# The second product of a token MLP: weight sums by additions alone, two of four made by an adding transfer

## The chip, the core and the metric

The kernel runs on one core of a Trainium2 chip. The core has a matrix engine (TensorE, PE in the profile, with its weight loads as PEld), a vector engine (VectorE, DVE), an activation engine (ScalarE, ACT), a general one (GpSimd, POOL) and SyncE (SP), which here only issues DMAs. Each engine takes its instructions in order and waits on semaphores for the others. SBUF is the on-chip memory with 128 partitions, PSUM the one into which PE accumulates. The metric is the device time of one execution in microseconds.

## The reference, cut to what matters

```python
def _B_ref(x, w1, b1, w2, b2):
    h = _layernorm(x, axis=-1)                       # (B, S, D)
    u = jnp.einsum("bsd,sf->bdf", h, w1) + b1        # (B, D, F)
    u = _gelu(u)
    y = jnp.einsum("bdf,fs->bds", u, w2) + b2        # (B, D, S)
    return y.transpose(0, 2, 1)

h = x + _A_ref(_layernorm(x), A_wqkv, A_w_phi, A_wo)     # attention
h2 = h + _B_ref(_layernorm(h), B_w1, B_b1, B_w2, B_b2)   # token MLP
```

Here S = 2048 tokens, D = 512 channels, F = 1792 hidden units, all in float32. The change is in the second product of the MLP, `u @ w2`.

## The kernel before, in words

The attention comes first, then the first product of the MLP (w1, lines 62 to 64 through `fill`), then the second (w2, line 789). All large products are made from float32 numbers split into two parts: `split` (lines 55 to 58) lets ACT round a tile to a high part (line 57) and another engine subtract it to get a low part (line 58); three matmuls then take the place of one (high by high, high by low, low by high).

The second product uses a scheme with seven block products in place of eight. The blocks are 2 x 2: the hidden units are taken in NP = 7 pairs of 128 (index `p`), the tokens in 8 pairs of 128 (index `sp`), the channels in two halves HD = 256. For each `sp` and `p` (one of 56 steps, `STEPS`, line 763) the four 128 x 128 blocks of w2 and their sums make seven weight tiles, `raw[:, i, 0]` to `raw[:, i, 6]`. The operands from `u` have their own sums, made once (`operands_u`, lines 729 to 749; for the first two `p` on POOL). `PROD` (line 784) says which weight tile meets which operand and in which of four PSUM banks the product is added. A step is 7 products of 3 matmuls.

`stream_w2` (lines 767 to 781) brings the weights of GRP = 2 steps, a group, so there are 28 groups: two loads from SP's queue (line 773), four additions or subtractions on DVE (lines 777 to 780), and a split of all seven tiles of both steps at once, ACT for `whi`, DVE for `wlo` (lines 57 and 58 through line 781). `raw` has three buffers, `whi` and `wlo` two each. The additions are kept behind one of the last low parts of w1 (`issue_after`, line 776).

After the seventh step of an `sp`, ACT and DVE combine the four banks (lines 820 to 826) into `ot`, and POOL's queue issues two transfers that add the rows to `out` in memory (line 827), which already holds `h`. The last `sp` adds in SBUF instead (`hb`, lines 830 to 847) and stores plainly.

The attention and the first part of w1's product keep an order written out by hand. From there on (line 697 closes the hand-kept stretch) the order on each engine is not written by hand: a planner lays them out when the program is built, by its own estimate of when each becomes ready. Each engine then keeps that order, whatever the real times are. The buffers of a tile are reused only after the last reader of the former content.

Of the kernel before, what the change touches and what calls it, by code (L numbers as in the profile page):

```python
# [9 lines left out]
F32 = mybir.dt.float32  # L10
F32R = mybir.dt.float32r
AF = mybir.ActivationFunctionType
ALU = mybir.AluOpType
# [4 lines left out]
P = 128  # L18
S, D, H, DH, F = 2048, 512, 32, 16, 1792
NT = S // P  # L20
KD = D // P
NF = F // P
NG = 8
NPR = 2 * NG
Q_AT = (4, 6, 8, 9, 11, 13)
# [8 lines left out]
def block_kernel(ctx: ExitStack, tc: tile.TileContext, x, xT, wT, phic, wo, w1, b1, w2, b2,  # L34
                 kvmask, ident_in, out):
    nc = tc.nc
# [7 lines left out]
    mhalf = cst.tile([P, 4], F32, name="mhalf")  # L44
    b1s = cst.tile([P, NF], F32, name="b1s")
    b2s = cst.tile([P, NT], F32, name="b2s")
# [41 lines left out]
    wvl = wp.tile([P, KD, D], F32R, name="wvl")  # L88
    zacc = wp.tile([P, NG, P], F32, name="zacc")
    ps_k = a1.enter_context(tc.tile_pool(name="ps_k", bufs=2, space=PSUM))  # L90
# [75 lines left out]
    def run(*lists):  # L166
        for op in turns(*lists):
            op()
# [7 lines left out]
    def k_ops(t, o):  # L176
        PK[t] = kk.tile([P, NG, P], F32, name="pk", bufs=len(V_NOT) + 3)
        run(logit_ops(o, PK[t], False))
# [187 lines left out]
    def q_logits(lag):  # L366
        n = q["logits"]
        if n < min(NT, q["mm"] - lag + NT * (q["mm"] == NT)):
            EQ[n] = big.tile([P, NG, P], F32, name="eq", tag="big")
            q["logits"] += 1  # L370
# [28 lines left out]
    for t in range(3, NT - 1):  # L399
        if t + 2 < NT:  # L400
            raw = load_x(t + 2)
# [38 lines left out]
    def s_ez(t):  # L440
        EZ[t] = az.tile([P, NG, P], F32, name="ez")
        nc.gpsimd.tensor_mul(EZ[t], EQ[t], zB)  # L442
# [40 lines left out]
    negate()  # L483
    zB = big.tile([P, NG, P], F32, name="zB", tag="big")
    for g in range(2):
# [106 lines left out]
        split(HN[t][:, 0], HN[t][:, 1], hn, nc.gpsimd)  # L592

    w1v = w1.rearrange("(k p) f -> p k f", p=P)
    w2v = w2.rearrange("(k p) s -> p k s", p=P)

    LATER = []

# [15 lines left out]
    PU, WI, LO = {}, {}, []  # L614
    FN, FL = [0] * (NF // 2), [0] * (NF // 2)

# [90 lines left out]

    NP = NF // 2  # L710
    HD = D // 2
    up = ctx.enter_context(tc.tile_pool(name="up", bufs=1, side="right", reuse_waits="tile"))
    uo = ctx.enter_context(tc.tile_pool(name="uo", bufs=2, side="right", reuse_waits="tile"))
    ws = ctx.enter_context(tc.tile_pool(name="ws", bufs=2, side="right", reuse_waits="tile"))
# [3 lines left out]
    NEAR = 2  # L718
    near = [up.tile([P, 7, 2, HD], F32R, name=f"un{p}") for p in range(NEAR)]
    up.tile([P, 120], F32, name="pad")  # L720
    U, UB, far = {}, {}, {}

    def gelu(f, pu):
        if f % 2 == 0:
            U[f // 2] = ur.tile([P, 4, HD], F32, name="u")
        nc.scalar.activation(U[f // 2][:, f % 2 * 2:f % 2 * 2 + 2].rearrange("p k d -> p (k d)"), pu,
                             AF.Gelu_apprx_tanh, bias=b1s[:, f:f + 1])

    def operands_u(p):
        u = U[p]  # L730
        tt = ut.tile([P, 3, HD], F32, name="tt")
        e = nc.gpsimd if p < NEAR else nc.vector
# [11 lines left out]
        for m in range(7):  # L744
            at = (p - NEAR) * 7 + m
            if at % 2 == 0:
                far[at // 2] = big.tile([P, 2, 2, HD], F32R, name="uf", tag="big")
            UB[p, m] = far[at // 2][:, at % 2]
            split(UB[p, m][:, 0], UB[p, m][:, 1], u[:, m] if m < 4 else tt[:, m - 4], nc.vector)

    for p in range(NP):
        while FN[p] < NT:
# [3 lines left out]
        if p < NEAR:  # L756
            operands_u(p)
    for p in range(NEAR, NP):
        operands_u(p)
    wst.close()  # L760
    hp = ctx.enter_context(tc.tile_pool(name="hp", bufs=1, reuse_waits="tile"))

    STEPS = [(sp, p) for sp in range(NT // 2) for p in range(NP)]
    GRP = 2
    AW = {}

    def stream_w2(n):
        steps = STEPS[n:n + GRP]
        raw = ws.tile([P, GRP, 7, P], F32, name="wraw", bufs=3)
        wh_ = ws.tile([P, GRP, 7, P], F32R, name="whi")  # L770
        wl_ = ws.tile([P, GRP, 7, P], F32R, name="wlo")
        for i, (sp, p) in enumerate(steps):
            nc.sync.dma_start(raw[:, i, 0:4].rearrange("p (k i) s -> p k (i s)", k=2),
                              w2v[:, 2 * p:2 * p + 2, sp * 2 * P:(sp + 1) * 2 * P])
            AW[sp, p] = wh_[:, i], wl_[:, i]
        with tc.issue_after(LO[-18]):
            nc.vector.tensor_add(raw[:, :, 4], raw[:, :, 0], raw[:, :, 2])
            nc.vector.tensor_sub(raw[:, :, 0], raw[:, :, 1], raw[:, :, 0])
            nc.vector.tensor_sub(raw[:, :, 5], raw[:, :, 4], raw[:, :, 1])
            nc.vector.tensor_sub(raw[:, :, 6], raw[:, :, 3], raw[:, :, 5])  # L780
        split(wh_, wl_, raw, nc.vector)


# [7 lines left out]
    def products(sp, ps, order):  # L791
        for a, b, bk, half, opens in order:
            for p in ps:
                wh_, wl_ = AW[sp, p]
                product(bank[bk][:, half], (wh_[:, a], wl_[:, a]), UB[p, b], p == 0 and opens, p == NP - 1)

    def flat(a):
        return a.rearrange("p k d -> p (k d)")

    for n, (sp, p) in enumerate(STEPS):  # L800
        t = 2 * sp
        last = t + 2 == NT
        if n % GRP == 0:
            stream_w2(n)
        if p == 0:
            pools = [ps_f, ps_f, ps_q, ps_q] if sp % 2 else [ps_b] * 4
            bank = [pool.tile([P, 2, HD], F32, name="py", tag="pu") for pool in pools]
        if p < NP - 1 - last:
            products(sp, [p], PROD)
            continue  # L810
        if p < NP - 1:
            continue
        by_bank = sorted(PROD, key=lambda m: m[2:4])
        e = uo.tile([P, 2, HD], F32, name="e")
        u2 = uo.tile([P, HD], F32, name="u2", bufs=1)
        u3 = uo.tile([P, HD], F32, name="u3")
        if not last:
            products(sp, [p], by_bank)
            ot = uo.tile([P, 2, 2, HD], F32, name="ot", bufs=1)
            nc.scalar.activation(e[:, 1], bank[0][:, 0], AF.Copy)  # L820
            nc.vector.tensor_add(u2, bank[0][:, 1], e[:, 1])
            nc.vector.tensor_add(u3, bank[1][:, 0], u2)
            nc.vector.tensor_add(e[:, 0], bank[2][:, 0], u2)
            for i, add in enumerate((u3.unsqueeze(1).to_broadcast([P, 2, HD]), e)):
                nc.vector.scalar_tensor_tensor(ot[:, i], bank[2 + i], b2s[:, t + i:t + i + 1], add,  # L825
                                               op0=ALU.add, op1=ALU.add)
                nc.gpsimd.dma_start(out[(t + i) * P:(t + i + 1) * P, :], flat(ot[:, i]), accum_op=ALU.add)  # L827
            continue

        hb = [hp.tile([P, 2, HD], F32, name=f"hb{i}") for i in range(2)]  # L830
        for i in range(2):
            nc.sync.dma_start(flat(hb[i]), out[(t + i) * P:(t + i + 1) * P, :])
            nc.vector.tensor_scalar(hb[i], hb[i], b2s[:, t + i:t + i + 1], None, op0=ALU.add)
        products(sp, [p - 1, p], by_bank)
        nc.scalar.activation(e[:, 1], bank[0][:, 0], AF.Copy)
        nc.vector.tensor_add(hb[1][:, 1], bank[0][:, 0], hb[1][:, 1])
        nc.vector.tensor_add(u2, bank[0][:, 1], e[:, 1])
        nc.vector.tensor_add(hb[1][:, 0], u2, hb[1][:, 0])
        nc.vector.tensor_add(u3, bank[1][:, 0], u2)
        nc.vector.tensor_add(hb[0], hb[0], u3.unsqueeze(1).to_broadcast([P, 2, HD]))  # L840
        nc.vector.tensor_add(hb[0][:, 0], bank[2][:, 0], hb[0][:, 0])
        nc.vector.tensor_add(hb[1][:, 0], bank[2][:, 0], hb[1][:, 0])
        nc.vector.tensor_add(hb[0][:, 1], bank[2][:, 1], hb[0][:, 1])
        nc.sync.dma_start(out[t * P:(t + 1) * P, :], flat(hb[0]))
        for k, q in ((0, nc.scalar), (1, nc.sync)):
            nc.vector.tensor_add(hb[1][:, k], bank[3][:, k], hb[1][:, k])
            q.dma_start(out[(t + 1) * P:NT * P, k * HD:(k + 1) * HD], hb[1][:, k])


def _layout(A_x, A_wqkv, A_w_phi, A_wo, B_w1, B_b1, B_w2, B_b2):  # L850
    x = np.asarray(A_x)[0]
    wqkv = np.asarray(A_wqkv)
    phi = np.asarray(A_w_phi)

    phic = np.concatenate([phi.reshape(4, P, DH).transpose(1, 0, 2).reshape(P, 64),
                           np.kron(np.eye(8), np.ones((DH, 1)))], axis=1).astype(np.float32)
    mask = np.zeros((P, 64), np.float32)
    for a in range(P // DH):
        for c in range(2):
            f = (2 * c + a % 2) * DH  # L860
            mask[a * DH:(a + 1) * DH, f:f + DH] = 1.0

    wo = np.asarray(A_wo).reshape(2, 4, 2, 32, D).transpose(2, 0, 1, 3, 4).reshape(D, D)
    return {
        "x": x,
        "xT": x.reshape(NT, P, KD, P).transpose(0, 3, 2, 1),
        "wT": wqkv.T,
        "phic": phic,
        "wo": wo,
        "w1": np.asarray(B_w1),  # L870
        "b1": np.asarray(B_b1).reshape(NF, P).T,
        "w2": np.asarray(B_w2),
        "b2": np.asarray(B_b2).reshape(NT, P).T,
        "kvmask": mask,
        "ident": np.eye(P, dtype=np.float32),
    }
# [18 lines left out]
```

## Time and profile before

| | |
|---|---|
| median of 3 runs | 534.46 us (534.25 to 535.26) |
| span of the profiled execution, first to last instruction | 532.6 us |
| second product's matmuls begin, busy without a gap | 386.0 us, 138.25 us |
| PE, DVE, ACT, POOL busy, of the span | 98%, 72%, 51%, 44% |
| DMA traffic | 55.81 MB, 105 GB/s on average |
| adding stores of `out` from POOL's queue | 14 of 256 KB, 4.8 us to landing |

The profile is of one execution; the runs are timed without it, and the difference of 1.8 us between the median and the span lies before the first and behind the last instruction. A row of a group reads: line, engine, operation, output<-inputs by the program's names, shapes, count, then busy time and mean duration in ns, then the engine's idle time just before, with what ended it. A row of the timeline begins with start and duration in us; a bracket at its end tells of idle time before it and what ended that. "A <- B: x, n, m" in the waits says that A waited for B for x us in all, n times, m at the longest. Queue q1 is SP's, q0 POOL's; a queue's row has packets, MB and the time its packets took as a share of the time of all 16 DMA engines.

### The profile page before, as it was taken

To read this page: it belongs to the slowest core of one execution; us is meant where nothing else is said; L and a number is where in the kernel's file an instruction comes from. 1 tells how busy PE (TensorE), PEld (TensorE's weight loads), DVE (VectorE), ACT (ScalarE), POOL (GpSimd) and SP (SyncE) were. 2 spreads that over 40 slices of the span, in tenths; PEclk is the share of its full clock that TensorE was granted. 3 is DMA by queue.
4 is the path that set the end of the run, shared out by engine and by line. 5 is a ranking of instruction groups with operands and counts; after the bars stand their busy time and mean duration, and the time that the engine had idled before them with its cause. 6 is when DMAs were issued, how large, how long until landed. Compare 5 with 4: busy or idle time off the path is not lost.

```text
span 532.6 us, 9386 instructions
## 1 busy us (share of the span) xinstructions
PE 520.8 (98%) x3616; PEld 448.7 (84%) x3616; DVE 384.4 (72%) x680; ACT 271.9 (51%) x460; POOL 234.8 (44%) x190
## 2 busy tenths in 40 slices
PE   8999999999999989999999999999999999999995
PEld 7888888886877767777788888888899999999995
DVE  6993999877699989875325524835668877887784
ACT  6998844424336776557746423525444243343340
POOL 2589699877889988887325000000001101100110
PEclk9999999999999999999999999999999999999999
DMA  8633310020502233334255333542014556535631
GB/s 309 206 110 118 99 22 21 1 72 9 160 0 79 82 101 116 104 116 136 85 176 159 98 100 98 159 117 82 20 41 107 143 148 153 123 120 136 143 75 46
DMA packets 45486, 55.81 MB, mean 105 GB/s; under 512 B 3969, under 2 KB 33025, under 8 KB 45441
## 3 DMA queue, kind: packets, MB, share of 16 engines
q1 hardware_dynamic: 43136, 51.38, 30.7%
q0 software_dynamic: 2016, 3.67, 5.5%
q8 instruction: 28, 0.46, 0.4%
q10 hardware_dynamic: 288, 0.17, 0.1%
q14 instruction: 18, 0.14, 0.1%
HBM read 46.81 MB, written 8.39 MB: 104 GB/s over the span
## 4 chain that ended last, share of the span: by engine, by line
PE 83%; POOL 9%; DVE 3%; ACT 2%; issue 1%; DVEq 0%; POOLq 0%; ACTq 0%
PE py L789 26%; PE pu L62 11%; PE pu L63 11%; PE pu L64 11%; POOL ez L442 4%; POOL eq L460 3%; PE pv L63 2%; PE pv L64 2%; PE pv L62 2%; PE pk_ps L62 2%; PE pk_ps L63 2%; PE pk_ps L64 2%; POOL hs L58 2%; PE po L62 1%; PE kvp L207 1%; PE po L63 1%
## 5 line engine op out<-in xcount | busy, mean ns | idle before, releaser
L827 POOL DMA_DIRECT2D out<-ot x14 | 12.5, 1001 | 212.2 <-DVE ot L825 212.2
L789 PE MATMUL py<-uf,whi 128*128 128x256 f32 x560 | 96.2, 283 | 0.0
L63 PE MATMUL pu<-hs,whi 128*128 128x512 f32 x224 | 87.6, 391 | 1.8 <-POOL hs L58 1.8
L602 DVE TENSOR_TENSOR wlo<-wraw,whi 128x512 fp32r<-128x512 f32 x56 | 50.3, 903 | 51.8 <-ACT whi L610 50.7
L57 ACT ACTIVATE whi<-wraw 128x1792 fp32r<-128x1792 f32 x28 | 47.7, 1705 | 77.9 <-PE py L789 73.8
L62 PE MATMUL pu<-hs,whi 128*128 128x512 f32 x224 | 87.4, 395 | 0.0
L64 PE MATMUL pu<-hs,wlo 128*128 128x512 f32 x224 | 87.2, 390 | 0.0
L789 PEld LDWEIGHTS py<-uf,whi 128*128 128x128 f32 x560 | 83.3, 192 | 0.0
L789 PE MATMUL py<-uf,wlo 128*128 128x256 f32 x280 | 69.9, 283 | 0.0
L58 DVE TENSOR_TENSOR wlo<-wraw,whi 128x1792 fp32r<-128x1792 f32 x28 | 56.6, 2022 | 15.4 <-ACT whi L57 15.4
L610 ACT ACTIVATE whi<-wraw 128x512 fp32r<-128x512 f32 x56 | 35.0, 627 | 47.0 <-PE pu L63 44.8
L63 PEld LDWEIGHTS pu<-hs,whi 128*128 128x128 f32 x224 | 42.1, 188 | 11.0 <-POOL hs L58 2.8
L62 PEld LDWEIGHTS pu<-hs,whi 128*128 128x128 f32 x224 | 42.0, 188 | 10.9 <-issue 2.5
L64 PEld LDWEIGHTS pu<-hs,wlo 128*128 128x128 f32 x224 | 42.0, 188 | 9.1 <-DVE wlo L602 0.4
L789 PEld LDWEIGHTS py<-uf,wlo 128*128 128x128 f32 x280 | 49.7, 192 | 0.0
L442 POOL TENSOR_TENSOR ez<-eq,zB 128x1024 f32<-128x1024 f32 x16 | 40.9, 2559 | 2.5 <-ACT zB L488 2.5
L789 PE MATMUL py<-un,whi 128*128 128x256 f32 x224 | 38.4, 283 | 0.0
L195 POOL TENSOR_TENSOR pk<-pk,sk 128x1024 f32<-128x1024 f32 x16 | 31.0, 1941 | 9.8 <-DVE sk L194 9.0
L460 POOL TENSOR_TENSOR eq<-eq,w 128x1024 f32<-128x1024 f32 x16 | 32.0, 1997 | 4.0 <-DVE w L457 4.0
L789 PEld LDWEIGHTS py<-un,whi 128*128 128x128 f32 x224 | 33.2, 192 | 0.1
L199 POOL TENSOR_TENSOR zacc<-zacc,pk 128x1024 f32<-128x1024 f32 x13 | 31.3, 2405 | 0.6
L58 POOL TENSOR_TENSOR hs<-hn,hs 128x512 fp32r<-128x512 f32 x16 | 21.4, 1340 | 17.5 <-ACT hs L57 15.6
(165 smaller groups left out, 1176.5 us busy)
## 6 DMA issues: line engine op xcount, KB each, us to landing
wraw<-in_w SPq DMA_DIRECT2D x112, 256.0 KB, 2.9
xraw<-in_xT SPq DMA_DIRECT2D x16, 256.0 KB, 3.1
xh<-in_x SPq DMA_DIRECT2D x16, 256.0 KB, 2.6
h<-in_x SPq DMA_DIRECT2D x16, 256.0 KB, 2.7
out<-h SPq DMA_DIRECT2D x16, 256.0 KB, 3.0
out<-ot POOLq DMA_DIRECT2D x14, 256.0 KB, 4.8
wraw<-in_wT SPq DMA_DIRECT2D x12, 256.0 KB, 5.0
wo<-in_wo SPq DMA_DIRECT2D x4, 256.0 KB, 3.6
```

The lines of the kernel that those rows point to most:

```text
L57: nc.scalar.activation(hi, src, AF.Copy)
L58: lo_engine.tensor_sub(lo, src, hi)
L62: nc.tensor.matmul(o, ah, bh, start=first, stop=False)
L63: nc.tensor.matmul(o, ah, bl, start=False, stop=False)
L64: nc.tensor.matmul(o, al, bh, start=False, stop=last)
L195: nc.gpsimd.tensor_mul(heads(PK[t]), heads(PK[t]), sk.unsqueeze(2).to_broadcast([P, 2 * H, DH]))
L199: nc.gpsimd.tensor_add(zacc, zacc, PK[t])
L442: nc.gpsimd.tensor_mul(EZ[t], EQ[t], zB)
L460: nc.gpsimd.tensor_mul(heads(EQ[t]), heads(EQ[t]), W[t].rearrange("p g c h -> p (g c h)").unsqueeze(2).to_broadcast([P, 2 * H, DH]))
L602: LO.append(nc.vector.tensor_sub(wl_, raw, wh_).ins)
L610: nc.scalar.activation(wh_, raw, AF.Copy)
L789: nc.tensor.matmul(o, a[x], b[:, y], start=start and i == 0, stop=stop and i == 2, skip_group_check=True)
```

## The change

The sums of weights are formed with other signs, so that all four are additions; the signs are turned back where the banks are combined. Two of the four sums are no longer made by DVE: an adding transfer, issued from POOL's queue, reads blocks 1 and 2 of w2 again from memory and adds them to tiles 0 and 4 in SBUF, after SP's queue has loaded block 0 a second time into tile 4. w2 is laid out in memory beforehand so that a group is one piece of 4 KB in each partition, `raw` has the two steps side by side in its last dimension and a fourth buffer, and the space set aside for the descriptors of POOL's queue is given as 8192.

```diff
 def stream_w2(n):
-    steps = STEPS[n:n + GRP]
-    raw = ws.tile([P, GRP, 7, P], F32, name="wraw", bufs=3)
-    wh_ = ws.tile([P, GRP, 7, P], F32R, name="whi")
-    wl_ = ws.tile([P, GRP, 7, P], F32R, name="wlo")
-    for i, (sp, p) in enumerate(steps):
-        nc.sync.dma_start(raw[:, i, 0:4].rearrange("p (k i) s -> p k (i s)", k=2),
-                          w2v[:, 2 * p:2 * p + 2, sp * 2 * P:(sp + 1) * 2 * P])
-        AW[sp, p] = wh_[:, i], wl_[:, i]
+    g = n // GRP
+    raw = ws.tile([P, 7, GRP * P], F32, name="wraw", bufs=4)
+    wh_ = ws.tile([P, 7, GRP * P], F32R, name="whi")
+    wl_ = ws.tile([P, 7, GRP * P], F32R, name="wlo")
+    nc.sync.dma_start(raw[:, 0:4], w2[g])
+    nc.sync.dma_start(raw[:, 4], w2[g, :, 0])
+    nc.gpsimd.dma_start(raw[:, 0:5:4], w2[g, :, 1:3], accum_op=ALU.add)
+    for i, step in enumerate(STEPS[n:n + GRP]):
+        AW[step] = wh_[:, :, i * P:(i + 1) * P], wl_[:, :, i * P:(i + 1) * P]
     with tc.issue_after(LO[-18]):
-        nc.vector.tensor_add(raw[:, :, 4], raw[:, :, 0], raw[:, :, 2])
-        nc.vector.tensor_sub(raw[:, :, 0], raw[:, :, 1], raw[:, :, 0])
-        nc.vector.tensor_sub(raw[:, :, 5], raw[:, :, 4], raw[:, :, 1])
-        nc.vector.tensor_sub(raw[:, :, 6], raw[:, :, 3], raw[:, :, 5])
+        nc.vector.tensor_add(raw[:, 5], raw[:, 4], raw[:, 1])
+        nc.vector.tensor_add(raw[:, 6], raw[:, 3], raw[:, 5])
     split(wh_, wl_, raw, nc.vector)
...
         nc.scalar.activation(e[:, 1], bank[0][:, 0], AF.Copy)
-        nc.vector.tensor_add(u2, bank[0][:, 1], e[:, 1])
-        nc.vector.tensor_add(u3, bank[1][:, 0], u2)
-        nc.vector.tensor_add(e[:, 0], bank[2][:, 0], u2)
+        nc.vector.tensor_sub(u2, bank[0][:, 1], e[:, 1])
+        nc.vector.tensor_sub(u3, u2, bank[1][:, 0])
+        nc.vector.scalar_tensor_tensor(e[:, 0], bank[2][:, 0], -1.0, u2, op0=ALU.mult, op1=ALU.subtract)
...
     nc.vector.tensor_add(hb[1][:, 1], bank[0][:, 0], hb[1][:, 1])
-    nc.vector.tensor_add(u2, bank[0][:, 1], e[:, 1])
-    nc.vector.tensor_add(hb[1][:, 0], u2, hb[1][:, 0])
-    nc.vector.tensor_add(u3, bank[1][:, 0], u2)
+    nc.vector.tensor_sub(u2, bank[0][:, 1], e[:, 1])
+    nc.vector.tensor_sub(hb[1][:, 0], hb[1][:, 0], u2)
+    nc.vector.tensor_sub(u3, u2, bank[1][:, 0])
...
-    nc.vector.tensor_add(hb[1][:, 0], bank[2][:, 0], hb[1][:, 0])
+    nc.vector.tensor_sub(hb[1][:, 0], hb[1][:, 0], bank[2][:, 0])
...
+    w2 = np.asarray(B_w2).reshape(NP, 2, P, NT // 2, 2, P).transpose(3, 0, 2, 1, 4, 5)
+    w2 = w2.reshape(-1, GRP, P, 4, P).transpose(0, 2, 3, 1, 4).reshape(-1, P, 4, GRP * P)
...
-    nc = bacc.Bacc("TRN2", target_bir_lowering=False, num_devices=1)
+    nc = bacc.Bacc("TRN2", target_bir_lowering=False, num_devices=1, dynamic_dma_scratch_size=8192)
```

More of the change, by code (lines that the diff above doesn't have):

```diff
@@ L22 @@
 NF = F // P
+NP = NF // 2
+HD = D // 2
+GRP = 2
 NG = 8
@@ L594, in block_kernel @@
     w1v = w1.rearrange("(k p) f -> p k f", p=P)
-    w2v = w2.rearrange("(k p) s -> p k s", p=P)
     LATER = []
@@ L699, in block_kernel @@
     aq.close()
-    NP = NF // 2
-    HD = D // 2
     up = ctx.enter_context(tc.tile_pool(name="up", bufs=1, side="right", reuse_waits="tile"))
@@ L763, in block_kernel @@
     STEPS = [(sp, p) for sp in range(NT // 2) for p in range(NP)]
-    GRP = 2
     AW = {}
     def stream_w2(n):
-        steps = STEPS[n:n + GRP]
-        raw = ws.tile([P, GRP, 7, P], F32, name="wraw", bufs=3)
-        wh_ = ws.tile([P, GRP, 7, P], F32R, name="whi")
-        wl_ = ws.tile([P, GRP, 7, P], F32R, name="wlo")
-        for i, (sp, p) in enumerate(steps):
-            nc.sync.dma_start(raw[:, i, 0:4].rearrange("p (k i) s -> p k (i s)", k=2),
-                              w2v[:, 2 * p:2 * p + 2, sp * 2 * P:(sp + 1) * 2 * P])
-            AW[sp, p] = wh_[:, i], wl_[:, i]
+        g = n // GRP
[7 more added lines that the diff above has]
+            AW[step] = wh_[:, :, i * P:(i + 1) * P], wl_[:, :, i * P:(i + 1) * P]
         with tc.issue_after(LO[-18]):
-            nc.vector.tensor_add(raw[:, :, 4], raw[:, :, 0], raw[:, :, 2])
-            nc.vector.tensor_sub(raw[:, :, 0], raw[:, :, 1], raw[:, :, 0])
-            nc.vector.tensor_sub(raw[:, :, 5], raw[:, :, 4], raw[:, :, 1])
-            nc.vector.tensor_sub(raw[:, :, 6], raw[:, :, 3], raw[:, :, 5])
+            nc.vector.tensor_add(raw[:, 5], raw[:, 4], raw[:, 1])
+            nc.vector.tensor_add(raw[:, 6], raw[:, 3], raw[:, 5])
         split(wh_, wl_, raw, nc.vector)
@@ L871, in _layout @@
         "b1": np.asarray(B_b1).reshape(NF, P).T,
-        "w2": np.asarray(B_w2),
+        "w2": w2,
         "b2": np.asarray(B_b2).reshape(NT, P).T,
```

## The prediction

> **What bounds the kernel now.** I read the page's busy shares first, then the chain of work that ended last in order of time, then the busy time by stretches.
>
> ```profile
> span 532.6 us, 9386 instructions
> PE 520.8 (98%) x3616; PEld 448.7 (84%) x3616; DVE 384.4 (72%) x680; ACT 271.9 (51%) x460; POOL 234.8 (44%) x190
> 385.99 138.25 PE py L789 x1152
> 386.00:524.30 138.30, 138.30 (x1154) 138.30 (x1154) 106.83 (x166) 50.06 (x43) 12.48 (x14) 1.00 0.48 115
> 524.30:532.60 8.30, 2.80 (x24) 2.60 (x22) 3.96 (x10) 0.35 (x1) 0.00 (x0) 0.90 0.18 64
> ```
>
> The columns of the last two rows are the stretch, its length, the busy time of PE, weight loads, DVE, ACT and POOL, then granted clock, busy share of the 16 DMA engines and GB/s. The second product is the chain's row at 385.99: 1152 matmuls in 138.25 us, 0.120 us each, PE busy all through at a granted clock of 1.00. DVE has 31 us to spare there, POOL 126. Nothing taken from DVE can shorten this stage; the change can leave it alone or make PE wait. A step has 7 x 3 = 21 matmuls, a group of two steps 42, so 5.04 us; an `sp` has 7 steps, 17.6 us or 3.5 groups. Group g starts at 386 + 5.04 g.
>
> How the weights are fed is seen in the waits of that stretch and in the order of DVE:
>
> ```profile
> ACT whi L57 <- PE py L789: 73.8, 25, 3.3
> DVE wraw L777 <- DMA wraw<-in_w: 11.5, 7, 3.3
> ```
>
> ```profile
> 335.17 2.02 DVE L58 TENSOR_TENSOR wlo<-wraw,whi 128x1792 fp32r<-128x1792 f32 x1 [0.50 <-ACT whi L57]
> ...
> 392.68 2.03 DVE L58 TENSOR_TENSOR wlo<-wraw,whi 128x1792 fp32r<-128x1792 f32 x1 [1.68 <-ACT whi L57]
> ...
> 412.89 2.03 DVE L58 TENSOR_TENSOR wlo<-wraw,whi 128x1792 fp32r<-128x1792 f32 x1 [0.93 <-ACT whi L57]
> 416.40 0.43 DVE L777 TENSOR_TENSOR wraw<-wraw 128x256 f32<-128x256 f32 x1 [1.49 <-DMA wraw<-in_w]
> ...
> 418.00 2.02 DVE L58 TENSOR_TENSOR wlo<-wraw,whi 128x1792 fp32r<-128x1792 f32 x1
> ```
>
> ACT rounds a group's weights to `whi` only when PE has left the buffer of two groups before; DVE makes `wlo` behind it and so frees `raw`. The first `wlo` here is that of group 0; the next three are those of groups 2, 6 and 7. The one that ends at 414.92 is 1.3 us ahead of group 6 (416.24). At 416.40 DVE stood 1.49 us in front of the sums of group 8, waiting for their load, with the `wlo` of group 7 queued behind. That cost nothing, because its `whi` was only just ready; a longer way to the sums makes just this wait longer.
>
> **The change part by part.** *Work on DVE.* A group loses two of its four sums.
>
> ```profile
> L777 DVE TENSOR_TENSOR wraw<-wraw 128x256 f32<-128x256 f32 x23 | 9.7, 421 | 11.6 <-DMA wraw<-in_w 11.5
> L821 DVE TENSOR_TENSOR u<-py,e 128x256 f32<-128x256 f32 x7 | 2.9, 417 | 0.0
> L825 DVE SCALAR_TENSOR_TENSOR ot<-py,b2s,u 128x512 f32<-128x512 f32 x7 | 5.2, 744 | 0.0
> ```
>
> Two at 0.42 us are 0.84 us a group, 23.5 us over 28 groups, all beside a PE that is never idle: worth 0. The turned signs at the end of an `sp` put a subtraction for an addition of the same size (0.417); the one new form with a scalar lies between 0.42 and the 0.744 of twice the columns, at most 0.33 x 7 = 2.3 us of DVE's spare time. That is also its price if the cover were gone. Behind the last matmul there are as many operations as before: 0.
>
> *Transfers.* SP issued two loads of 256 KB a group and now issues one of 512 and one of 128 KB, again two, so nothing more stands ahead of w1's loads in its queue. New is the adding transfer of 256 KB from POOL, which waits for both. DMA time is priced from the page's queues:
>
> ```profile
> q1 hardware_dynamic: 43136, 51.38, 30.7%
> q0 software_dynamic: 2016, 3.67, 5.5%
> 394.73 113.64 SPq L773 DMA_DIRECT2D wraw<-in_w  x46
> L827 POOL DMA_DIRECT2D out<-ot x14: 858/1075/1227, 408.1 to 515.1; - x14
> wraw<-in_w SPq DMA_DIRECT2D x112, 256.0 KB, 2.9
> h<-in_x SPq DMA_DIRECT2D x16, 256.0 KB, 2.7
> ```
>
> SP's queue: 30.7% of 532.6 us is 163.5 us of all 16 engines for 51.38 MB, 3.18 us a MB. POOL's queue carries only the 14 adding stores: 29.3 us, 2.09 us for each 256 KB, 2.5 times a plain byte. The prices fit the stretch: 46 loads x 0.262 MB x 3.18 + 29.3 = 67.7 of 138.3 us, 0.49, where the window shows 0.48.
>
> After the change a group loads 0.655 MB: 2.08 us. Its adding transfer is not in the trace. By bytes it costs what the stores do, 2.09; but it moves rows of 1 KB, twice as many pieces, so up to 4.18. Plain loads by pieces of 1 KB (`wraw`, 2.9 us to landing) and of 2 KB (`h`, 2.7) hardly differ, so I go a third of the way up: 2.79. Groups 0 to 3 find a free `raw` at the start (one more than now), 4 and 5 are loaded once the first two `wlo` are done, from 337 on and well ahead of 386; groups 6 to 27, 22 of them, from the `wlo` that ends at 394.7. The last must have landed by 516.2: `whi` of group 27 may start when group 25 ends (517.0), 0.84 of sums before it. So in 121.5 us: 22 x (2.08 + 2.79) + 6 pairs of stores x 4.18 = 107.1 + 25.1 = 132.2 us. That is 10.7 us more than there is. Low end 22 x 4.17 + 25.1 = 116.8, which fits, 0; high end 22 x 6.26 + 25.1 = 162.8, +41.3.
>
> The Trainium skill (DMA: Bandwidth & Descriptors, "Issuing engines are not separate DMA queues") says that transfers of every issuing engine end on the same 16 DMA engines and interleave. The landing rows below agree, 3.0 us free against 5.6 beside stores. Were POOL's queue a road of its own, SP's share alone would be 22 x 2.08 = 45.8 of 121.5 us, and the sum would be 0; by the rule it is the one above.
>
> *POOL's queue.* One adding transfer a group at 0.86 to 1.23 us by the stores' row, double if pieces count: 28 to 69 us beside 126 idle. Behind a waiting one only the stores of `out` are queued, which have 17.6 us until `ot` is written again. The first four stand near POOL's work on `u`:
>
> ```profile
> 273.45 1.30 POOL L58 TENSOR_TENSOR hs<-hn,hs 128x512 fp32r<-128x512 f32 x1 [1.97 <-DMA wraw<-in_w]
> ...
> 289.92 1.68 POOL L736 TENSOR_TENSOR tt<-u,tt 128x256 f32<-128x256 f32 x1
> 274.78 2.93 SPq L773 DMA_DIRECT2D wraw<-in_w  x6
> ```
>
> The last `hs`, for which PE would wait, is done before the first load is issued at 274.78, and `u` of POOL is wanted at 386, 94 us later: 0; uncovered, four issues, 4 to 10 us. The halved space for POOL's descriptors is given up for the fourth `raw`; nothing in the trace prices it, and a POOL that waited for space would lengthen the way below, no more.
>
> *The way to the sums.* Landings, in turn, of the loads at 394.7 and 410.4 and of the stores at 408.1:
>
> ```profile
> 394.73 0.89 SPq L773 DMA_DIRECT2D wraw<-in_w  x2
> DMA to landing us min/median/max: 2.5/2.8/3.0
> 410.40 0.90 SPq L773 DMA_DIRECT2D wraw<-in_w  x2
> DMA to landing us min/median/max: 5.3/5.4/5.6
> DMA to landing us min/median/max: 4.0/5.3/6.6
> ```
>
> A pair is there 3.4 us after the first issue when DMA is free (second issue 0.4 later, 3.0) and 6.0 beside stores. With 0.4 for the added bytes and a store's 4.0 or 6.6 for the adding transfer, `raw` is ready for DVE 7.8 us after it was freed, 13.0 beside stores; before it was 3.4 and 6.0. Then come 0.84 of sums and 2.03 of `wlo`. The fourth buffer allows 3 x 5.04 = 15.1 us if the planner puts the sums of group g+4 behind the `wlo` of g+2 on DVE, so 12.2 for the way: mostly enough, and I add nothing for it.
>
> **Sum.** 0 from DVE, 0 from POOL, +10.7 from DMA engines that have more to do than the stage has time. The execution's span is 532.6; 1.8 us lie around it up to the median 534.46. 532.6 + 10.7 + 1.8 = 545.1.
>
> **Rivals.** *Hidden.* The four buffers decide, at L769: if the adding transfer costs 2.3 us of engine time or less (22 x 4.38 + 25.1 = 121.5) and the way stays under 12.2, PE never sees it. For it: rows of 4 KB for the large load, and 0.0 idle on PE today although DVE waits 11.5 us for loads. Against: 0.96 of the time even at the low end. Time 534.4. The Trainium skill (DMA: Bandwidth & Descriptors, "Anatomy of one DMA — SWDGE (gpsimd) path") gives 2.0 us + bytes / 436e3 for a transfer from GpSimd, an estimated 2.6 us here; by it the way is 6.4 and this rival wins. The stores' 4.0 to 6.6 do not agree.
>
> *The wait on DVE takes its place.* If the planner puts the sums of g+4 ahead of the `wlo` of g+2, as it put those of group 8 ahead of 418.00, two groups take way + 2.87: 10.7 free (5.3 a group, +0.3) and 15.9 beside stores (7.9, +2.9). Over 22 groups that is +6.6 to, with two of 3.5 groups beside stores, 22 x (2 x 2.9 + 1.5 x 0.3) / 3.5 = +39; the middle is 557. Against it: before, the sums came right behind a `wlo`, not into a gap.
>
> *Faster.* DVE's lighter load would have to show at the end, 524.3 to 532.6, the only part from 386 on where PE is not full; 1.5 us off gives 533.0. Against it: DVE idles there until ACT's first copy.
>
> ```profile
> 524.68 0.42 DVE L836 TENSOR_TENSOR hb<-py,hb 128x256 f32<-128x256 f32 x1 [3.92 <-ACT e L835]
> ```
>
> **Numbers.** Forecast 545, 0.43, own range 535.5 to 560; hidden 0.33; DVE's wait 0.19; faster 0.05. A measurement of this kernel can tell 0.2%, 1.1 us, from no change. So slower 0.62, same 0.33, faster 0.05. The range from 533.8 takes in the hidden case and goes to 563; above lie the dear half of DVE's wait and the forecast's high end, below the faster case, together under 0.2.
>
> **What would show it.** DMA share in the second product at 0.85 or more; PE idle ahead of `py`, ended by `wlo`; DVE's wait in front of its first sum (now 11.5 us) put down to the adding transfer; that transfer landing in 4 to 7 us. A share below 0.75 with PE still at 0.120 us a matmul means hidden. PE waits with a share below 0.75 mean the wait on DVE. PE idle before 386 would make all of it wrong.

## The result and the profile after

The changed kernel takes 576.54 us (median of 4 runs, 574.42 to 578.41) against 534.43 us: 1.0782 times the time before, 95% interval 1.0756 to 1.0808. It is 42.1 us slower; 545 was forecast, in a range up to 563. The profiled execution has a span of 574.9 us, 42.3 more than before. In two of the experiments below one run was far longer than the others, 2943.58 and 1044.76 us at a full clock, and the medians given there leave it out (with it they are 534.08 and 547.44).

The page shows what moved. First the busy shares, the DMA queues, the chain that ended last, two of the groups and the transfers of the weights (size, median us to landing):

```profile
span 574.9 us, 9429 instructions
PE 535.0 (93%) x3616; PEld 460.2 (80%) x3616; DVE 365.8 (64%) x624; ACT 271.2 (47%) x460; POOL 267.9 (47%) x218
q1 hardware_dynamic: 35968, 55.05, 30.7%
q0 software_dynamic: 9632, 11.01, 13.3%
PE 58%; DMA 19%; POOL 9%; DVE 8%; issue 3%; ACT 3%; SPq 0%; DVEq 0%; POOLq 0%; ACTq 0%
L787 PE MATMUL py<-uf,wlo 128*128 128x256 f32 x280 | 75.2, 303 | 21.8 <-DVE wlo L61 21.7
L777 DVE TENSOR_TENSOR wraw<-wraw 128x256 f32<-128x256 f32 x28 | 11.6, 423 | 81.4 <-DMA wraw<-in_w 81.4
wraw<-in_w SPq DMA_DIRECT2D x28, 512.0 KB, 4.7
wraw<-in_w POOLq DMA_DIRECT2D x28, 256.0 KB, 6.0
wraw<-in_w SPq DMA_DIRECT2D x28, 128.0 KB, 4.8
```

DVE is busy for 18.6 us less and the kernel got slower: the chain now runs for 19% through transfers. DVE's wait in front of its first sum grew from 11.6 to 81.4 us, and PE, which never waited in this product, waits for `wlo`.

Where the second product's time went is one window from its start to the place of the same last matmuls (columns as in the prediction's windows):

```profile
386.00:566.90 180.90, 152.54 (x1153) 149.70 (x1152) 90.35 (x118) 49.78 (x41) 39.35 (x36) 0.92 0.62 133
```

180.9 us in place of 138.3: PE is idle for 28.4 of them, and the same matmuls are busy 14.2 us longer. The granted clock is 0.92 here; before it was 1.00. By PE's own account two thirds of the loss are waiting and one third is a slower PE; how much of that third sets the time is answered at the end of the part on the prediction. The DMA engines are busy for 0.62 of the time, less than in the forecast, which wanted them full.

The order on DVE tells why PE waits. Three stretches of its timeline, then SP and POOL for the group that comes next in the same buffer:

```profile
404.91 0.43 DVE L777 TENSOR_TENSOR wraw<-wraw 128x256 f32<-128x256 f32 x1 [5.26 <-DMA wraw<-in_w]
405.37 0.42 DVE L778 TENSOR_TENSOR wraw<-wraw 128x256 f32<-128x256 f32 x1
405.71 2.02 DVE L61 TENSOR_TENSOR wlo<-wraw,whi 128x1792 fp32r<-128x1792 f32 x1
...
411.37 2.02 DVE L61 TENSOR_TENSOR wlo<-wraw,whi 128x1792 fp32r<-128x1792 f32 x1
420.25 0.43 DVE L777 TENSOR_TENSOR wraw<-wraw 128x256 f32<-128x256 f32 x1 [6.86 <-DMA wraw<-in_w]
420.71 0.43 DVE L778 TENSOR_TENSOR wraw<-wraw 128x256 f32<-128x256 f32 x1
421.05 2.02 DVE L61 TENSOR_TENSOR wlo<-wraw,whi 128x1792 fp32r<-128x1792 f32 x1
```

```profile
407.75 0.33 SPq L771 DMA_DIRECT2D wraw<-in_w  x1
408.13 0.46 SPq L772 DMA_DIRECT2D wraw<-in_w  x1
```

```profile
413.59 1.21 POOL L773 DMA_DIRECT2D wraw<-in_w  x1 [1.31 <-DMA wraw<-in_w]
```

The low parts at 405.71, 411.37 and 421.05 are those of groups 4, 5 and 6. When `wlo` of group 4 ends at 407.73, its `raw` is free, and SP issues the loads of group 8 at 407.75. POOL issues the adding transfer at 413.59, when both have landed, and it lands at 420.2. Only then, 12.5 us after the buffer was freed, do the sums of group 8 start, at 420.25. They stand in front of the low part of group 6, whose `whi` had been ready since 413.74. PE gets that low part at 423.07 and has run dry:

```profile
417.74 1.00 PE L787 MATMUL py<-uf,whi 128*128 128x256 f32 x7
423.12 1.01 PE L787 MATMUL py<-uf,wlo 128*128 128x256 f32 x3 [4.38 <-DVE wlo L61]
```

This is the second rival of the prediction: the sums of g+4 ahead of the `wlo` of g+2, so that two groups cost one way (from the freed `raw` to its sums) plus 2.87 us. Over the 22 groups from group 6 on I take the way from the timeline as the time from the end of a `wlo` to the start of the sums four groups on: 11.3 us on average, 9.1 to 14.1. (11.3 + 2.87) / 2 = 7.1 us a group in place of 5.04, times 22 is +45; measured +42.

### The profile page after: what moved, and what is told of

It reads as the page before. It is cut to its first block, busy times and chain, and to the rows that moved or that the text cites. A ratio compares the mean times of both kernels' runs of the same rounds, so it can differ in the third digit from the quotient of the medians.

```text
span 574.9 us, 9429 instructions
## 1 busy us (share of the span) xinstructions
PE 535.0 (93%) x3616; PEld 460.2 (80%) x3616; DVE 365.8 (64%) x624; ACT 271.2 (47%) x460; POOL 267.9 (47%) x218
## 3 DMA queue, kind: packets, MB, share of 16 engines
q0 software_dynamic: 9632, 11.01, 13.3%
## 4 chain that ended last, share of the span: by engine, by line
PE 58%; DMA 19%; POOL 9%; DVE 8%; issue 3%; ACT 3%; SPq 0%; DVEq 0%; POOLq 0%; ACTq 0%
DMA wraw<-in_w 18%; PE pu L65 10%; PE pu L66 10%; PE pu L67 10%; PE py L787 6%; DVE wlo L61 4%; POOL ez L445 3%; POOL eq L463 2%; PE pv L66 2%; PE pv L67 2%; PE pv L65 2%; PE pk_ps L65 2%; PE pk_ps L67 2%; PE pk_ps L66 2%; POOL hs L61 2%
## 5 line engine op out<-in xcount | busy, mean ns | idle before, releaser
L773 POOL DMA_DIRECT2D wraw<-in_w x28 | 36.2, 1294 | 203.7 <-DMA wraw<-in_w 148.2
L787 PE MATMUL py<-uf,whi 128*128 128x256 f32 x560 | 101.4, 293 | 0.0
L787 PE MATMUL py<-uf,wlo 128*128 128x256 f32 x280 | 75.2, 303 | 21.8 <-DVE wlo L61 21.7
L787 PEld LDWEIGHTS py<-uf,whi 128*128 128x128 f32 x560 | 88.2, 203 | 0.0
L787 PEld LDWEIGHTS py<-uf,wlo 128*128 128x128 f32 x280 | 53.6, 208 | 24.1 <-DVE wlo L61 24.1
L777 DVE TENSOR_TENSOR wraw<-wraw 128x256 f32<-128x256 f32 x28 | 11.6, 423 | 81.4 <-DMA wraw<-in_w 81.4
L66 PEld LDWEIGHTS pu<-hs,whi 128*128 128x128 f32 x224 | 42.1, 188 | 11.0 <-POOL hs L61 2.7
L65 PEld LDWEIGHTS pu<-hs,whi 128*128 128x128 f32 x224 | 42.1, 188 | 10.8 <-issue 2.5
L787 PE MATMUL py<-un,whi 128*128 128x256 f32 x224 | 41.2, 296 | 0.0
L787 PE MATMUL py<-un,wlo 128*128 128x256 f32 x112 | 29.8, 305 | 6.5 <-DVE wlo L61 6.5
L787 PEld LDWEIGHTS py<-un,whi 128*128 128x128 f32 x224 | 35.9, 206 | 0.1
```

The lines of the kernel that those rows point to most:

```text
L65: nc.tensor.matmul(o, ah, bh, start=first, stop=False)
L66: nc.tensor.matmul(o, ah, bl, start=False, stop=False)
L773: nc.gpsimd.dma_start(raw[:, 0:5:4], w2[g, :, 1:3], accum_op=ALU.add)
L787: nc.tensor.matmul(o, a[x], b[:, y], start=start and i == 0, stop=stop and i == 2, skip_group_check=True)
```

## The experiments

Two theories stood against each other. "Place": the sums wait for a long way and stand too early in DVE's queue. "Engines", the forecast's: the DMA engines have more to move than the stage has time for. Eight kernels ran.

**The place alone, moved behind the low part just before, and behind that of two groups before.** The edits to the changed kernel; the second has 2 for 1:

```diff
+    W2LO = []
...
-        with tc.issue_after(LO[-18]):
+        with tc.issue_after(W2LO[-1] if g >= 1 else LO[-18]):
...
-        split(wh_, wl_, raw, nc.vector)
+        nc.scalar.activation(wh_, raw, AF.Copy)
+        W2LO.append(nc.vector.tensor_sub(wl_, raw, wh_).ins)
```

> The changed kernel with one edge more: on DVE the two sums of a group are issued behind the low part of the group just before it (they stood ahead of the low part two groups before). All transfers stay. Theory 'place': the loss comes from the sums standing ahead of a low part that is wanted sooner; a raw buffer's round then has 4 groups (20.2 us) for a way of 10 to 12.5 us plus 2.87, so PE runs without a gap, 534 to 536 us, granted clock 1.0 up to the end. Theory 'engines' (the forecast's): the 16 DMA engines have too little time, the order on DVE does not matter, the time stays above 560 and DVE's or ACT's wait for the adding transfer stays near 75 us.

> The same edge, but behind the low part of two groups before, one place later than in the changed kernel. Theory 'place': a round has 3 groups, 15.1 us, for way + 2.87 = 13 to 15.4 us, so nearly enough: 535 to 543 us with some gaps on PE near the adding stores. Theory 'engines': above 560 us as before.

Behind the group just before: 534.02 us, 0.9988 times the kernel before (0.9979 to 0.9998); all 42 us are gone with every transfer still there. Behind two before: 546.76 us, 1.0219 times (1.0185 to 1.0254), a little above what was expected. The two windows of the second product, in that order, and DVE's order in the first kernel:

```profile
386.00:524.30 138.30, 138.30 (x1154) 138.30 (x1153) 92.02 (x124) 50.10 (x42) 39.49 (x36) 1.00 0.77 174
```

```profile
386.00:534.10 148.10, 140.26 (x1151) 138.37 (x1151) 90.99 (x122) 49.94 (x42) 39.38 (x36) 1.00 0.75 162
```

```profile
413.01 2.03 DVE L781 TENSOR_TENSOR wlo<-wraw,whi 128x1792 fp32r<-128x1792 f32 x1 [2.21 <-ACT whi L780]
414.96 0.42 DVE L778 TENSOR_TENSOR wraw<-wraw 128x256 f32<-128x256 f32 x1
415.41 0.42 DVE L779 TENSOR_TENSOR wraw<-wraw 128x256 f32<-128x256 f32 x1
418.05 2.03 DVE L781 TENSOR_TENSOR wlo<-wraw,whi 128x1792 fp32r<-128x1792 f32 x1 [2.22 <-ACT whi L780]
```

In the first, PE is full and the DMA engines are busy for 0.77 of the time, more than the slow kernel's 0.62, in a shorter stage. DVE waits for `whi` again and its sums find their transfer landed: nothing is idle in front of them. In the second PE is idle for 7.8 us, and the clock stays at 1.00; this execution is the shortest of its kernel, 544.14 us, and the next two have a mean clock of 0.993. One place in one queue is worth 30 us, a second one 13.

**The bytes without the wait.** The adding transfer goes to a tile that nobody reads.

```diff
+    SINK = [hp.tile([P, 2, GRP * P], F32, name=f"sink{i}") for i in range(2)]
+    for s in SINK:
+        nc.gpsimd.memset(s, 0.0)
...
-        nc.gpsimd.dma_start(raw[:, 0:5:4], w2[g, :, 1:3], accum_op=ALU.add)
+        sink = SINK[g % 2]
+        nc.gpsimd.tensor_copy(sink[:, 0, 0:1], raw[:, 4, 0:1])
+        nc.gpsimd.dma_start(sink, w2[g, :, 1:3], accum_op=ALU.add)
```

> The changed kernel, but the adding transfer of each group goes into one of two tiles that nobody reads (after POOL has copied one column of the loaded raw, so that it still follows the loads); tiles 0 and 4 keep block 0 alone, so two of the four sums are left out. The same bytes move at the same pace, and nothing waits for the adding transfer. Theory 'place' (it is the wait for its landing that costs): 534 to 540 us. Theory 'engines': the load on the DMA engines is the same, so above 560 us.

Measured 535.29 us, 1.002 times (1.0003 to 1.0037). Its window has the highest DMA share of all the runs:

```profile
386.00:524.30 138.30, 137.93 (x1145) 137.42 (x1144) 91.81 (x122) 50.40 (x42) 46.62 (x66) 1.00 0.80 182
```

The bytes are the same, but a row of the sink is one piece of 2 KB where the changed kernel has two of 1 KB, so POOL's queue has 6048 packets in place of 9632. A share of 0.80 at 182 GB/s costs PE 0.4 us. "Engines" has fallen.

**No second load and no adding transfer.**

```diff
-        nc.sync.dma_start(raw[:, 4], w2[g, :, 0])
-        nc.gpsimd.dma_start(raw[:, 0:5:4], w2[g, :, 1:3], accum_op=ALU.add)
...
+            nc.vector.tensor_add(raw[:, 4], raw[:, 0], raw[:, 2])
+            nc.vector.tensor_add(raw[:, 0], raw[:, 0], raw[:, 1])
             nc.vector.tensor_add(raw[:, 5], raw[:, 4], raw[:, 1])
```

> The changed layout, the one load of 512 KB, four raw buffers and the turned signs, but no second load and no adding transfer; all four sums are additions on DVE again. Both theories: 534.4 within 1 us, since two additions of 0.42 us a group are beside a full PE; more than that would put part of the loss on the layout or the signs.

Measured 534.26 us, 0.9996 times (0.9986 to 1.0005). Layout, signs, the fourth buffer and the descriptor space cost nothing, the last with the adding transfers too, as the first experiment shows; and two additions fewer on DVE (534.02 us there) give nothing that this measurement tells from it.

**Is it the adding?** One argument less, and every engine's order is the changed kernel's:

```diff
-        nc.gpsimd.dma_start(raw[:, 0:5:4], w2[g, :, 1:3], accum_op=ALU.add)
+        nc.gpsimd.dma_start(raw[:, 0:5:4], w2[g, :, 1:3])
```

> The changed kernel with a plain transfer from POOL's queue in place of the adding one: same bytes, same queue, same waits, every engine's order unchanged; blocks 1 and 2 overwrite tiles 0 and 4, so two of the four sums are left out. Theory 'place': a way of two transfers one behind the other is what the early place cannot bear. A plain piece of 1 KB takes less than an adding one, perhaps 1 us off a way of 10.7, so half a us a group: 562 to 574 us. If adding in the DMA engines is itself the cause, the loss falls by more than half, below 555 us.

Measured 560.38 us, 1.048 times (1.0442 to 1.0518), just below the range expected for "place", and above the 555 of the other answer. The transfer lands faster:

```profile
q0 software_dynamic: 4256, 11.01, 8.8%
wraw<-in_w POOLq DMA_DIRECT2D x28, 256.0 KB, 3.9
```

3.9 us to landing where the adding one took 6.0; the way, taken as above, is 10.0 us on average instead of 11.3. By the rule of two groups a way, (10.0 + 2.87) / 2 = 6.4 us, +30 over 22 groups; measured +26. So a second hop without adding makes more than half of the loss. The other 16 us are not the adding alone: POOL's queue has 4256 packets here in place of 9632, so the plain transfers went in larger pieces (4 KB in the trace, where the adding ones went in 1 KB), and not in the pieces of 1 KB that I had expected. Adding and smaller pieces were not tried apart.

**The early place with a short way.** The kernel with four sums on DVE, its loads and sums written two groups ahead, and each low part held behind the sums of two groups later:

```diff
+            SUMS2[g] = nc.vector.tensor_add(raw[:, 6], raw[:, 3], raw[:, 5]).ins
...
+        nc.scalar.activation(wh_, raw, AF.Copy)
+        with tc.issue_after(SUMS2[min(g + 2, len(STEPS) // GRP - 1)]):
+            nc.vector.tensor_sub(wl_, raw, wh_)
```

> The kernel with four sums on DVE and no adding transfer, but each low part is held behind the sums of two groups later, the place that the changed kernel has. Theory 'place': the place costs only together with a long way. Here the way is one load, 3.4 to 6 us, and two groups take way + 1.68 + 2.03 = 7.1 to 9.7 us, below 10.08: 534 to 536 us. If the place alone were the fault: above 545 us.

Measured 534.15 us, 0.9993 times (0.9984 to 1.0002). The place does no harm while the way is a single load.

The edge only pins what was there. The planner had given the kernel with four sums on DVE this order unasked, and the trace of this run has the same. These rows of the kernel with four sums are the low part of group 5, the first and the last sum of group 8, and the low part of group 6:

```profile
408.30 2.02 DVE L61 TENSOR_TENSOR wlo<-wraw,whi 128x1792 fp32r<-128x1792 f32 x1
410.23 0.42 DVE L775 TENSOR_TENSOR wraw<-wraw 128x256 f32<-128x256 f32 x1
...
411.48 0.42 DVE L778 TENSOR_TENSOR wraw<-wraw 128x256 f32<-128x256 f32 x1
412.78 2.03 DVE L61 TENSOR_TENSOR wlo<-wraw,whi 128x1792 fp32r<-128x1792 f32 x1 [0.88 <-ACT whi L60]
```

The sums of group 8 stand between the low parts of groups 5 and 6, as in the changed kernel. One kernel takes 534.26 us with that place and the other 576.54.

**Three buffers in the repaired order.** One number in the first experiment's kernel: `bufs=3` for `wraw`.

> The kernel with the sums behind the low part just before, but three raw buffers as there were before the change. Theory 'place': a buffer's round falls from 4 groups to 3, 15.1 us for way + 2.87 = 13 to 15.4 us, the same sum as for the sums one place earlier with four buffers (547.4 us): 538 to 552 us. If the fourth buffer is not needed once the place is right: 534 to 535 us.

Measured 549.25 us, 1.0254 times (1.0213 to 1.0295), inside the range, but partly by another road than I had said. Its waits:

```profile
ACT whi L780 <- DVE wraw L779: 87.3, 22, 6.0
DVE wlo L781 <- ACT whi L780: 36.8, 19, 2.3
DVE wraw L778 <- DMA wraw<-in_w: 20.2, 15, 2.9
```

Here it is ACT that waits for the sums of its own group (87.3 us): with one buffer less the weights come too late for `whi` itself. In this order the fourth buffer is needed.

**What a pause of PE costs.** On the kernel with four sums on DVE:

```diff
+        for _ in range(4 if g in (8, 11, 14, 17, 20, 23) else 0):
+            nc.scalar.activation(wh_, raw, AF.Copy)
         split(wh_, wl_, raw, nc.vector)
```

> What an idle PE costs by itself, on the kernel with four sums on DVE: in 6 groups ACT rounds the weights five times over, so whi ends 8.5 us and wlo 10.6 us after PE left the buffer; PE idles about 3.5 and 1.1 us each time, 27.6 us in all. Idle alone: 562 us. If a pause of this length brings the clock of 0.5 that the changed kernel shows for 3.4 to 6.8 us after its longest pauses, a further 1.7 to 3.4 us each, 572 to 582 us.

Measured 579.59 us, 1.084 times (1.0818 to 1.0862), in the range for a lower clock. Its window up to the last matmuls, and four windows around the first pause:

```profile
386.00:569.10 183.10, 154.51 (x1153) 151.15 (x1152) 106.73 (x162) 89.55 (x66) 12.42 (x14) 0.91 0.34 84
```

```profile
424.00:427.00 3.00, 3.00 (x26) 2.89 (x25) 1.88 (x5) 2.97 (x2) 1.74 (x2) 1.00 0.55 79
427.00:432.20 5.20, 0.20 (x2) 0.10 (x1) 0.12 (x1) 5.02 (x4) 0.00 (x0) 0.84 0.42 56
432.20:437.00 4.80, 4.80 (x21) 4.52 (x22) 3.84 (x2) 0.00 (x0) 0.00 (x0) 0.50 0.35 109
437.00:440.00 3.00, 3.00 (x26) 3.00 (x26) 1.65 (x5) 0.20 (x1) 0.00 (x0) 0.95 0.52 175
```

28.6 us idle, about the 27.6 that were put in, and 16.2 us more of busy time. After the pause 21 matmuls take 4.8 us, 0.23 each, at a clock of 0.50, before 0.12 returns. With the DMA share at 0.34 and no adding transfer, the same slow third appears as in the changed kernel: it follows from the pauses.

## Why the prediction was wrong

*What bounds the kernel, and DVE's lighter load worth nothing:* right. PE was full before, and the repaired kernel with two sums fewer is where the kernel before is. The sums that went from DVE took 23.4 us (23.5 was worked out; the page's busy time falls by 18.6, since it counts overlapping instructions once), and the one new form with a scalar took 0.42 us, no more than the addition did.

*Transfers, the term that made the forecast:* wrong. The step "107.1 + 25.1 = 132.2 us. That is 10.7 us more than there is" took 2.79 us of engine time for an adding transfer. In the repaired kernel POOL's queue takes

```profile
q0 software_dynamic: 9632, 11.01, 13.6%
```

13.6% of 532.2 us, 72.4. By the packets in that trace 47.7 us of it went to the 7168 pieces of 1 KB of the adding transfers and 24.0 to the 1792 pieces of 2 KB of the stores. That is 1.70 us for each of the 28 adding transfers, below the low end of my bounds (2.09). The demand is 22 x (2.08 + 1.70) + 25.1 = 108.3 of 121.5 us, and the engines have room. So "+10.7 from DMA engines that have more to do than the stage has time" is the sum's failed term.

*The way to the sums, the step that cost the most:* "The fourth buffer allows 15.1 us ... if the planner puts the sums of group g+4 behind the `wlo` of g+2 ...: mostly enough, and I add nothing for it." Both halves failed. The planner put them ahead of it, so that a round had two groups, 10.1 us, and not three; and even one place later the 15.1 us are not enough (546.76 us), because the loads took 5.4 and 6.1 us to landing in that run (median of the large and the small one), where I had 3.4 + 0.4 on a free road, and the adding transfer 6.3: 12.4 us with 12.2 allowed, before POOL's turn. The way there, taken as above, was 13.1 us on average. For the changed kernel the size was right: its 11.3 us lie between my 7.8 and 13.0.

*The rivals.* "The wait on DVE takes its place" is what happened, with its place, its rule and nearly its number: +39 was worked out, +42 measured. That it came so near is in part luck: the sum mixes ways of 7.8 and of 13.0 us, and the measured ones run from 9.1 to 14.1, none as short as 7.8. I gave the rival 0.19 and held against it that before, the sums had come right behind a `wlo`. That argument failed. In the kernel before, the sums of group 8 use the buffer of group 5 and stand behind the `wlo` of 6, ahead of that of 7. In the changed kernel they use the buffer of group 4 and stand behind the `wlo` of 5, ahead of that of 6. Counted from the low part that frees the buffer this is the same place, right behind the next low part and so ahead of the second. The planner moved nothing: it left the sums there for a way of one load and for a way of two transfers alike, and made no use of the fourth buffer for a later place. Why it did so is open. The prediction's own sign told this rival from the others: PE waits with a DMA share below 0.75, here 0.62. "Hidden" comes back when the sums stand two places later, as the first experiment shows. The estimate from the Trainium skill (DMA: Bandwidth & Descriptors, "Anatomy of one DMA — SWDGE (gpsimd) path") that spoke for it, 2.6 us for the adding transfer, is not what these runs show: 6.0 us beside other traffic and never under 4.0, and 3.9 for a plain one.

*POOL's queue, the first groups, the end of an `sp`:* the 0 holds. The second product starts within 0.1 us of where it did before (385.7), and with the place repaired the time is that of before. POOL's issue of the transfer took 1.19 us and more (1.29 on average), within 0.86 to twice 1.23; the low end of the 28 to 69 us for all 28 should have read 24, and 36.2 were measured.

*What the rivals left out:* the slower clock. It costs less than PE's account suggests. From 392 us to the end of the stage the chain that ended last comes through PE only twice:

```profile
492.40 10.88 PE py L787 x76
549.50 17.48 PE py L787 x131
```

The clock is at 0.5 in six spells, from 421.3, 448.6, 475.9, 493.0, 520.3 and 551.0 us on. Only the fourth and the last lie in these two rows, 3.4 us each at half the clock, so 3.4 us lost. During the other four the chain runs through transfers and DVE, and PE would have waited for them at full clock too. So most of the 14.2 us lies beside the wait, and the rule of two groups comes to +45 without any clock in it. This is read from the chain; the changed kernel was not run at a full clock.

## What to carry to other kernels

When work moves from an engine to a transfer, the engine's time saved is one number and the way from a freed buffer to the usable data another. Multiply out how many groups a buffer's round spans at the place where the consumer stands in its in-order queue, and compare with the way: here 2, 3 and 4 groups gave 576.5, 546.8 and 534.0 us with the same transfers. Where a planner lays out the queues, a long wait is worth pinning by hand behind the work that is wanted sooner.

## What the runs showed of the hardware

A pause of PE can cost more than itself: where PE sets the pace, as in the last experiment, 28.6 us of pauses brought 16.2 us more of busy time. In the changed kernel the granted clock falls to 0.5 during or just behind each of its six longest pauses; the window of the one at 418.5, of 4.7 us, with the seven us behind it:

```profile
412.00:421.00 9.00, 6.38 (x51) 5.97 (x50) 2.11 (x3) 3.40 (x2) 2.71 (x3) 1.00 0.82 159
421.00:428.00 7.00, 4.88 (x23) 4.88 (x24) 4.86 (x5) 0.38 (x1) 0.65 (x1) 0.52 0.61 150
428.00:435.00 7.00, 7.00 (x59) 7.00 (x59) 4.28 (x7) 2.08 (x2) 3.60 (x4) 0.99 0.96 176
```

From start to start of two matmuls those pauses are 2.49 to 6.46 us long, and 0.5 lasts 3.4 or 6.8 us. In the profiled execution with the sums behind two groups before, pauses of up to 2.11 us left the clock at 1.00, and with the plain copy those up to 2.35 us did. The length of one pause is not all, though: in the last experiment the clock fell to 0.5 behind two pauses of 1.97 and 2.37 us that begin 2.9 us apart. The Trainium skill (TensorE: Matmul & The Clock Gate, "Part 1: The HAM clock gate") says that PE goes to half its clock after at least one idle window of about 3.4 us; the steps of 3.4 us agree, but here a pause of 2.49 us was enough.

In the repaired kernel 256 KB took the DMA engines 1.70 us as an adding transfer into SBUF and 1.71 us as an adding store to memory (2.06 in the kernel before), though the first has twice as many pieces.
